# Block-causal attention with a SoLU MLP: transposed tiles placed in an order that alternates partition halves, queries and keys loaded for two head pairs at once, and W_out's rows permuted

## The chip, the cores and the metric

The kernel runs on one core of a Trainium2 chip. Its time is the device time of one execution in microseconds (us). The engines are PE (matrix products and transposes through the identity), DVE, ACT and POOL (elementwise work and reductions) and SP, whose only work here is to issue DMAs, one after the other, in the order of its queue.

## The reference

Attention over 8 batches, 8 heads, 576 positions of 64 channels, with a mask by blocks of 64; then, per token, an MLP with a SoLU and a layer norm. All is float32, and the weights are handed over as float64 words.

```python
scores = scale * np.matmul(q, k.transpose(0, 1, 3, 2))       # scale = 1/8
scores = np.where(block_i >= block_j, scores, -1000000000.0)
attn = softmax(scores)                                        # rows, with 1e-9 in the divisor
x = np.matmul(attn, v).transpose(0, 2, 1, 3).reshape(4608, 512)
h = x @ w_in                                                  # 512 -> 1024
solu = h * softmax(h)
ln = (solu - mean) / np.sqrt(var + 1e-06) * g_ln              # over the 1024
out = ln @ w_out                                              # 1024 -> 512
```

## The kernel before

**Tiling.** The 64 (batch, head) pairs are worked on two heads at a time: 32 "pairs" p, four to a batch. One head lies in partitions 0 to 63, the other in 64 to 127. After every batch the 128-token MLP tiles t that are complete are added, 36 in all. Products that need more than one pass of the reduced float32 format are split into a high and a low part: `qh, ql, kh, kl` for queries and keys, `wih, wil, woh, wol` for the weights, `xh, xl` and `ch, cl` for what the MLP multiplies.

**One pair.** Queries and keys come in raw as `qz, kz`. For pairs 0 to 3 PE transposes them; from pair 4 on (28 pairs) they are loaded as 32-column pieces of 128 bytes (L432, four DMAs for each of q and k), DVE transposes the 32x32 blocks into `qt, kt` (L474), ACT or POOL makes the high part (L475), DVE or POOL the low part (L478, L481). POOL copies the last block's queries into `qdh, qdl` (L485). PE makes the scores (L515, L509), DVE their row maxima (L540), ACT the exponentials into `pb` (L552), DVE the reciprocal sums (L562, L563), POOL or ACT the scaling (L570, L572). Then `pb` must be transposed: for pairs 0 to 3 by PE (L496), from pair 4 on by DVE in 32x32 blocks (L579) and sixteen DMAs (`place`, L584) that carry block row a of quarter r to quarter r of `pt`, 100 KB each. PE multiplies by the values (L596, the "AV" product, 52 matrix instructions a pair) into `xt`.

**One MLP tile.** Two groups of 12 matrix products with 512 columns (L673), maximum, exponential, product with h (L679 to L681), subtraction of the mean in place in `ub` (L683 on POOL or L684 on DVE), square sum (L685), then the transpose: for tiles 4 to 34 by DVE in 32x32 blocks into `zb` (L703), a DMA to DRAM (`zd`, L704) and one back (`ct`, L705); for tiles 0 to 3 and 35 by PE straight from `ub` (L721). High and low parts (L711 to L715), two groups of 12 products with W_out (L733), scaling (L737), the store (L739).

**Weights.** At the start sixteen pieces (eight of W_in, eight of W_out) are loaded as float64 words into `ub` (L345), turned into float32 and split (L347 to L365), with `zb`, `ct` and `ob` as scratch.

**What sets the order.** `Schedule.run` plans all engines at once: each operation has a duration, a priority out of `PARAMS`, and sometimes a choice of engines (`alts`); a list scheduler with slots for PSUM tiles gives one fixed order per engine. SP's queue is part of it: an operation of SP is a run of DMA issues with a time for the issue, `dma` (the time on the DMA engines, one after the other) and `tail`. On the chip each engine walks its order, waiting by semaphores alone.

## Time and profile before

| | |
|---|---|
| median of three runs | 729.7 us (728.79 to 730.06) |
| the profiled execution | 730.28 us, its span 728.5 us, mean granted TensorE clock 0.970 |
| PE, DVE, ACT, POOL busy | 671.1, 607.4, 495.3, 322.5 us |
| DMA | 125.49 MB, 231547 packets, 70.1% of 16 engines' span on SP's queue |
| `place` | 448 issues of 100 KB, 2.2 us to landing |
| q and k of pairs 4 to 31 | 224 issues of 72 KB, 3.0 and 2.7 us to landing |
| weights | 16 issues of 512 KB, 4.2 and 4.3 us to landing |

A busy PE is counted with matmul ends that are modelled, so that gaps in it are real but short stalls do not show. SP's issues do not count as busy time; how full SP is must be read from the order of its instructions in time.

### The profile page before, as it was taken

To read this page: it belongs to the slowest core of one execution; us is meant where nothing else is said; L and a number is where in the kernel's file an instruction comes from. 1 tells how busy PE (TensorE), PEld (TensorE's weight loads), DVE (VectorE), ACT (ScalarE), POOL (GpSimd) and SP (SyncE) were. 2 spreads that over 40 slices of the span, in tenths; PEclk is the share of its full clock that TensorE was granted. 3 is DMA by queue.
4 is the path that set the end of the run, shared out by engine and by line. 5 is a ranking of instruction groups with operands and counts; after the bars stand their busy time and mean duration, and the time that the engine had idled before them with its cause. 6 is when DMAs were issued, how large, how long until landed. Compare 5 with 4: busy or idle time off the path is not lost.

```text
span 728.5 us, 14348 instructions
## 1 busy us (share of the span) xinstructions
PE 671.1 (92%) x4543; PEld 528.1 (72%) x4543; DVE 607.4 (83%) x1262; ACT 495.3 (68%) x1265; POOL 322.5 (44%) x491
## 2 busy tenths in 40 slices
PE   7786968999999998999999999899899988999997
PEld 6566757777677776778777777677677766878886
DVE  6999999988888999789799888899888789755672
ACT  5989958877777777665777686578585658434342
POOL 3755744454444655244353654245454434214310
PEclk7899989999999999999999999999999999999999
DMA  9584676676788888888778888888787874543431
GB/s 236 130 175 118 150 178 117 126 170 146 161 201 201 205 196 193 198 192 210 182 193 197 203 196 173 190 199 196 193 209 178 190 197 110 170 151 130 145 131 57
DMA packets 231547, 125.49 MB, mean 172 GB/s; under 512 B 190640, under 2 KB 206512, under 8 KB 231472
## 3 DMA queue, kind: packets, MB, share of 16 engines
q1 hardware_dynamic: 230416, 124.32, 70.1%
q8 instruction: 36, 0.59, 0.4%
q10 hardware_dynamic: 1056, 0.26, 0.2%
q14 instruction: 39, 0.32, 0.2%
HBM read 52.96 MB, written 25.69 MB: 108 GB/s over the span
## 4 chain that ended last, share of the span: by engine, by line
PE 32%; DVE 23%; SPq 14%; DMA 12%; ACT 12%; issue 5%; POOL 1%; DVEq 0%; ACTq 0%; POOLq 0%
PE ps L733 12%; SPq L584 11%; PE ps L673 9%; PE ps L596 5%; DVE pb L579 5%; DVE nm L540 5%; DMA pt<-pb 4%; ACT pb L552 4%; PE ps L515 4%; DMA ct<-zd 3%; ACT pb L572 3%; SPq L432 2%; DVE ub L681 2%; DVE zb L703 2%; PE ps L509 1%
## 5 line engine op out<-in xcount | busy, mean ns | idle before, releaser
L552 ACT ACTIVATE pb<-ps,nm 128x384 f32<-128x384 f32 (+4 forms) x288 | 157.3, 561 | 69.6 <-DVE nm L540 54.2
L540 DVE TENSOR_REDUCE nm<-ps 128x1 f32<-128x384 f32 (+4 forms) x288 | 131.8, 506 | 0.3
L596 PE MATMUL ps<-pt,vr 128*64 128x128 f32 (+2 forms) x1664 | 104.3, 286 | 25.4 <-DMA pt<-pb 13.7
L596 PEld LDWEIGHTS ps<-pt,vr 128*64 128x64 f32 x1664 | 90.2, 146 | 46.9 <-issue 16.4
L572 ACT ACTIVATE pb<-pb,rz 128x128 f32<-128x128 f32 (+4 forms) x191 | 101.2, 595 | 25.4 <-DVE rz L563 23.0
L579 DVE STREAM_TRANSPOSE pb<-pb 128x1536 f32<-128x1536 f32 (+1 forms) x56 | 102.1, 1829 | 9.5 <-POOL pb L570 5.8
L570 POOL TENSOR_SCALAR pb<-pb,rz 128x384 f32<-128x384 f32 (+4 forms) x97 | 62.3, 652 | 71.3 <-DVE rz L563 30.4
L733 PE MATMUL ps<-woh,ch 128*128 128x512 f32 x288 | 81.6, 405 | 4.0 <-ACT pb L552 3.4
L673 PE MATMUL ps<-wih,xh 128*128 128x512 f32 x288 | 83.8, 413 | 0.2 <-ACT xh L648 0.2
L673 PE MATMUL ps<-wil,xh 128*128 128x512 f32 x288 | 79.4, 398 | 0.0
L733 PE MATMUL ps<-woh,cl 128*128 128x512 f32 x288 | 78.7, 395 | 0.0
L673 PE MATMUL ps<-wih,xl 128*128 128x512 f32 x288 | 78.6, 395 | 0.0
L733 PE MATMUL ps<-wol,ch 128*128 128x512 f32 x288 | 78.6, 394 | 0.0
L733 PEld LDWEIGHTS ps<-woh,ch 128*128 128x128 f32 x288 | 51.8, 188 | 20.2 <-ACT pb L552 5.6
L703 DVE STREAM_TRANSPOSE zb<-ub 128x1024 f32<-128x1024 f32 x31 | 62.5, 2017 | 2.6 <-POOL ub L683 1.4
L673 PEld LDWEIGHTS ps<-wil,xh 128*128 128x128 f32 x288 | 54.8, 190 | 13.0
L673 PEld LDWEIGHTS ps<-wih,xh 128*128 128x128 f32 x288 | 51.1, 190 | 17.3 <-issue 4.8
L673 PEld LDWEIGHTS ps<-wih,xl 128*128 128x128 f32 x288 | 54.3, 188 | 12.8
L733 PEld LDWEIGHTS ps<-woh,cl 128*128 128x128 f32 x288 | 54.3, 188 | 12.8
L515 PE MATMUL ps<-kh,qh 64*128 64x384 f32 (+3 forms) x256 | 57.8, 390 | 6.2 <-ACT pb L552 1.8
L733 PEld LDWEIGHTS ps<-wol,ch 128*128 128x128 f32 x288 | 54.2, 188 | 12.7
L712 POOL TENSOR_SCALAR ch<-ct 128x512 fp32r<-128x512 f32 x36 | 22.0, 620 | 90.0 <-DMA ct<-zd 77.0
(116 smaller groups left out, 1262.3 us busy)
## 6 DMA issues: line engine op xcount, KB each, us to landing
pt<-pb SPq DMA_DIRECT2D x448, 100.0 KB, 2.2
zd<-zb SPq DMA_DIRECT2D x31, 512.0 KB, 3.0
ct<-zd SPq DMA_DIRECT2D x31, 512.0 KB, 4.3
out_dram<-ob SPq DMA_DIRECT2D x36, 256.0 KB, 3.1
vr<-in_v_dram SPq DMA_DIRECT2D x64, 128.0 KB, 3.3
kz<-in_k_dram SPq DMA_DIRECT2D x112, 72.0 KB, 2.7
qz<-in_q_dram SPq DMA_DIRECT2D x112, 72.0 KB, 3.0
ub<-in_moe_w_in_dram SPq DMA_DIRECT2D x8, 512.0 KB, 4.2
```

Source lines behind the costliest of these rows:

```text
L515: PE.matmul(PS(sps[h])[:, off : off + 128 * (i_ + 1)], w_[half[h], 128 * i_ : 128 * i_ + 128], x_[half[h], 0 : 128 * (i_ + 1)], start=n_ = ...
L540: op("DVE", t_dve(wid[u]), lambda sp=sp, off=off, u=u: DVE.tensor_reduce(out=nm_[u], in_=PS(sp)[:, off : off + wid[u]], axis=AX.X, op=ALU. ...
L552: ACT.activation(dst, src, AF.Exp, bias=nm_[u], accum_out=z_[zg][:, zc : zc + 1])
L570: op("POOL", 0.836 * nn + 243, lambda b=b, zg=zg, zc=zc: POOL.tensor_scalar(out=puv(pb, b, pep), in0=puv(pb, b, pep), scalar1=rz_[zg][:, z ...
L572: ("ACT", t_act(nn, 93), lambda b=b, zg=zg, zc=zc: ACT.activation(puv(pb, b, pep), puv(pb, b, pep), AF.Copy, scale=rz_[zg][:, zc : zc + 1] ...
L579: op("DVE", 1.058 * 128 * (s1 - s0) + 86, lambda s0=s0, s1=s1: DVE.transpose(pb[:, :, s0:s1, :], pb[:, :, s0:s1, :]), r=[("P", i, b) for b ...
L584: SP.dma_start(pt_[32 * r_ : 32 * r_ + 32, a_, :, :], pb[32 * a_ : 32 * a_ + 32, r_, :, :])
L596: PE.matmul(dst(PS(av)[half[h]]), vt[:, j, 64 * h : 64 * h + 64], pt_[:, a0:a1, sl, :], start=start, stop=stop)
L673: PE.matmul(o_, a_[:, c, :], w_[:, c, s_], start=(si == 0 and c == 0), stop=(si == 2 and c == NKI - 1))
L703: op("DVE", t_dve(DFF), lambda: DVE.transpose(zb.rearrange("p (r c i) -> p r c i", r=4, i=32), u.rearrange("p (c i r) -> p r c i", r=4, i= ...
L712: alts=[("POOL", 671, lambda c_=c_, h_=h_: POOL.tensor_scalar(out=h_, in0=c_, scalar1=1.0, scalar2=1.0, op0=ALU.mult, op1=ALU.mult), K["a_ ...
L733: PE.matmul(o_, a_[:, c, :], w_[:, c, :], start=(hf == 0 and si == 0 and c == 0), stop=(hf == 1 and si == 2 and c == 7))
```

## The change

Five things change in the code, and all numbers of the planner with them, so that every engine's order is new.

1. **Loads of q and k.** `qz, kz` hold two pairs side by side. One DMA brings 32 columns of two heads: four DMAs of 144 KB for each of q and k per two pairs (L450), 112 issues in all where there were 224. To make the source regular, a pair is now heads 4a+z and 4a+z+2, so W_in's rows are permuted alike: its pieces are loaded in two halves of 64 partitions (`heads`, 16 issues for 8). The 32x32 transposes of q and k are done in place (`qt, kt` are gone): the next load of two pairs must wait until both pairs are through with the raw tile.
2. **Placing.** The sixteen DMAs of `place` are the same, in another order: source and target quarter now change between partitions 0-63 and 64-127 from one DMA to the next.
3. **W_out's rows.** They are loaded with rows r of four interleaved (`rows`, 32 issues for 8, and 4 for 1 of `gt`), so that the DVE transpose of the MLP reads 32 neighbouring elements where it read every fourth. For tiles 0 to 3 and 35, which PE transposes, the subtraction of the mean writes into `zb` in the permuted order; it waits, at tile 0, for all weights, whose scratch `zb` is.
4. **The planner.** A DMA now occupies the modelled DMA engines from its issue on, SP stops when more than 2.5 us are outstanding, `place` has 5.5 us on the DMA engines where it had 0.25, and three durations are larger.
5. **Choices of engine.** With the new numbers, POOL scales 156 of the `pb` blocks (97 before) and ACT 132 (191 before); POOL makes 34 of the 56 high parts of q and k, of which ACT made all; in the weights' preparation DVE makes 7 of the low parts (16 before) and none of the high parts (9 before), and 16 of the clamps (7 before).

```diff
-    "nd": 2, "ld": 63.8, "lv": 26.1, "q": -25.0, "qe": -924.4, ...
+    "nd": 2, "ld": 15.5, "lv": 976.7, "q": 13.1, "qe": 1200.3, ...
...
-                    done = dmafree = max(done, dmafree) + best.dma
+                    dmafree = max(t + min(best.dur, 600.0), dmafree) + best.dma
+                    engfree[e] = max(done, dmafree - DEPTH)
+                    done = max(engfree[e], dmafree)
...
-    qz, kz, qt, kt = (sb(x, [S]) for x in ("qz", "kz", "qt", "kt"))
+    qz, kz = (sb(x, [2, S]) for x in ("qz", "kz"))
...
-    w_in_w = w_in.bitcast(U32).rearrange("(c p) (n t) -> p c n t", p=P, t=2)
-    w_out_w = w_out.bitcast(U32).rearrange("(c p) (n t) -> p c n t", p=P, t=2)
+    w_in_w = w_in.bitcast(U32).rearrange("(a h z d) (n t) -> d a z h n t", h=2, z=2, d=64, t=2)
+    w_out_w = w_out.bitcast(U32).rearrange("(c r j) (n t) -> r j c n t", r=4, j=32, t=2)
...
+    def rows(dst, src):
+        for r_ in range(4):
+            SP.dma_start(dst[r_::4], src[r_])
+
+    def heads(dst, src):
+        for h in range(2):
+            SP.dma_start(dst[64 * h : 64 * h + 64], src[:, h])
...
-                for g in range(4):
-                    dma.dma_start(
-                        dst[32 * g : 32 * g + 32, :].rearrange("p (g d) -> p g d", d=32),
-                        src[b0, 2 * hp + g // 2, :, 32 * (g % 2) : 32 * (g % 2) + 32].rearrange("(g p) d -> p g d", p=32),
-                    )
+            def load2(nm=nm, src=src, dst=dst):
+                for g in range(4):
+                    SP.dma_start(
+                        dst[32 * g : 32 * g + 32].rearrange("p m (g d) -> p (m g) d", d=32),
+                        src[b0, ha + g - g % 2 : ha + g - g % 2 + 2, :, 32 * (g % 2) : 32 * (g % 2) + 32].rearrange("m (g p) d -> p (m g) d", p=32),
+                    )
...
+            elif zs == 0:
+                op("SP", 2600, load2, w=[(nm, 0), (nm, 1)], key=lk, tail=1700, dma=3740)
...
-            op("DVE", t_dve(S) + 30, lambda z=z, t=t: DVE.transpose(t, z), r=[x + "z"], w=[x + "t"], key=kk)
+            op("DVE", t_dve(S) + 30, lambda z=z: DVE.transpose(z, z), r=[zk], w=[zk], key=kk)
...
-            for r_ in range(4):
-                for a_ in range(4):
+            for d_ in (2, 3, 0, 1):
+                for a_ in (0, 2, 1, 3):
+                    r_ = a_ ^ d_
                     SP.dma_start(pt_[32 * r_ : 32 * r_ + 32, a_, :, :], pb[32 * a_ : 32 * a_ + 32, r_, :, :])
...
+        if not PET <= t < PEL:
+            dst, src = (x.rearrange("p (c a b) -> p c a b", a=a_, b=P // a_) for x, a_ in ((zb, 32), (u, 4)))
+            src = src.rearrange("p c r j -> p c j r")
+            cw, ck = ["zb"], "zb"
...
-            op("DVE", t_dve(DFF), lambda: DVE.transpose(zb.rearrange("p (r c i) -> p r c i", r=4, i=32), u.rearrange("p (c i r) -> p r c i", r=4, i=32)), ...
+            op("DVE", t_dve(DFF), lambda: DVE.transpose(zb.rearrange("p (r c i) -> p r c i", r=4, i=32), u.rearrange("p (c r i) -> p r c i", r=4, i=32)), ...
```

How SP's queue reads in the middle of the program, before. A row is a run of equal DMAs: line, what is written and read, the shape of one, how many. `pt<-pb` is `place`, `zd` and `ct` are the two halves of an MLP transpose, `vr` the values.

```order
L584 DMA pt_94<-pb_92 32x800 x16
L704 DMA zd<-zb 128x1024
L739 DMA out_dram<-ob_137 128x512
L432 DMA kz<-in_k_dram 32x18x32 x4
L432 DMA qz<-in_q_dram 32x18x32 x4
L705 DMA ct<-zd 128x4x256
L584 DMA pt_93<-pb_91 32x800 x16
L704 DMA zd<-zb 128x1024
L441 DMA vr_84<-in_v_dram 128x4x64 x2
L445 DMA vr_84<-in_v_dram 64x2x64
L739 DMA out_dram<-ob_138 128x512
L432 DMA kz<-in_k_dram 32x18x32 x4
```

The same place with the change, two pairs of `place` apart:

```order
L608 DMA pt_92<-pb_90 32x800 x16
L744 DMA zd<-zb 128x1024
L779 DMA out_dram<-ob_138 128x512
L450 DMA kz<-in_k_dram 32x36x32 x4
L745 DMA ct<-zd 128x4x256
L450 DMA qz<-in_q_dram 32x36x32 x4
L608 DMA pt_91<-pb_89 32x800 x16
L744 DMA zd<-zb 128x1024
L779 DMA out_dram<-ob_137 128x512
L463 DMA vr_82<-in_v_dram 128x4x64 x2
L467 DMA vr_82<-in_v_dram 64x2x64
L745 DMA ct<-zd 128x4x256
```

Eight issues of q and k now stand between every second pair of `place`, where eight stood between each two; the rest of a turn is as it was. The load stands ahead of a `place` in the queue.

The start of SP's queue, before (the keys of pair 0 go by ACT's queue):

```order
L345 DMA ub_128<-in_moe_w_in_dram 128x1024
L426 DMA kq<-in_k_dram 64x2x64
L421 DMA qz<-in_q_dram 128x4x64 x2
L426 DMA kq<-in_q_dram 64x2x64
L345 DMA ub_129<-in_moe_w_in_dram 128x1024
L441 DMA vr_83<-in_v_dram 128x4x64 x2
```

and with the change:

```order
L352 DMA ub_126<-in_moe_w_in_dram 64x1024 x2
L352 DMA ub_127<-in_moe_w_in_dram 64x1024 x2
L463 DMA vr_82<-in_v_dram 128x4x64 x2
L467 DMA vr_82<-in_v_dram 64x2x64
L463 DMA vr_81<-in_v_dram 128x4x64 x2
L467 DMA vr_81<-in_v_dram 64x2x64
L352 DMA ub_126<-in_moe_w_in_dram 64x1024 x2
L352 DMA ub_127<-in_moe_w_in_dram 64x1024 x2
L443 DMA kq<-in_k_dram 64x2x64
L438 DMA qz<-in_q_dram 128x4x64 x2
```

The queries of pair 0 stood behind two issues; now fifteen stand ahead of them, two of which reuse a weight buffer and so wait for its first piece to be read. On PE, 28 groups of 12 MLP products stand behind the last AV product before, and 33 with the change.

More of the change, by code (lines that the diff above doesn't have):

```diff
@@ L33 @@
 PEP = (0, 1, 2, 3)
+DRP = ()
+PDMA = 5500
 PET, PEL = 4, 35
@@ L38 @@
 SWITCH = 70.0
+DEPTH = 2500.0
 SLACK = 120.0
@@ L278 @@
     zd = dp.tile([P, DFF], F32, name="zd")
+    pd = [dp.tile([P, 4, NSL * 32], F32, name=f"pd{i}") for i in range(2)]
     ct = sb("ct", [4, NKO, 32])
@@ L344, in prep @@
         kr_, k1, k2, k3 = ("ub", i % 2), ("w1", i % 2), ("w2", i % 2), ("ob", i % 2)
-        op("SP", 640, lambda: SP.dma_start(raw, src), w=[kr_], key=key, tail=2700, dma=1270)
+        if gcol is None:
+            op("SP", 2 * 640, lambda: heads(raw, src), w=[kr_], key=key, tail=2700, dma=1270)
+        else:
+            op("SP", 4 * 640, lambda: rows(raw, src), w=[kr_], key=key, tail=2700, dma=1270)
         high = raw[:, :, 1].bitcast(F32)
@@ L372 @@
             s_ = slice(hf * 512, hf * 512 + 512)
[L373 removed]
+            prep(n, w_in_w[:, c // 2, c % 2, :, s_, :], wih[:, c, s_], wil[:, c, s_], None, f"wi{c}_{hf}", K["w0"] + K["w1"] * n)
             n += 1
     for c in range(NKO):
[L376 removed]
+        prep(n, w_out_w[:, :, c], woh[:, c, :], wol[:, c, :], gt[:, c : c + 1], f"wo{c}", K["w0"] + K["w1"] * n)
         n += 1
@@ L414, in attention, with load @@
         pep = p in PEP
+        zs = p % 2
+        ha = 4 * (hp // 2) + zs
         for nm, src, dst in (("kz", k, kz), ("qz", q, qz)):
-            def load(nm=nm, src=src, dst=dst):
+            def load(nm=nm, src=src, dst=dst[:, zs]):
                 dma = ACT if p == 0 and nm == "kz" else SP
-                if peq:
-                    for h in range(2):
-                        dma.dma_start(
-                            dst[:, 0:512].rearrange("p (c d) -> p c d", c=4)[:, :, 64 * h : 64 * h + 64],
-                            src[b0, 2 * hp + h, 0:512, :].rearrange("(c p) d -> p c d", p=P),
-                        )
-                    r0 = 0 if nm == "kz" else 64
+                for h in range(2):
+                    dma.dma_start(
+                        dst[:, 0:512].rearrange("p (c d) -> p c d", c=4)[:, :, 64 * h : 64 * h + 64],
+                        src[b0, ha + 2 * h, 0:512, :].rearrange("(c p) d -> p c d", p=P),
+                    )
+                r0 = 0 if nm == "kz" else 64
+                SP.dma_start(
+                    kq[r0 : r0 + 64, :].rearrange("p (h d) -> p h d", h=2),
+                    src[b0, ha : ha + 3 : 2, 512:576, :].rearrange("h p d -> p h d"),
+                )
+            def load2(nm=nm, src=src, dst=dst):
+                for g in range(4):
@@ L521, in attention @@
             else:
-                d, md = sum(3 * t_row(128 * (i_ + 1)) for i_, _ in us) + {1: 0, 2: 48, 3: 74}[us[0][0]], 2
+                d, md = sum(3 * t_row(128 * (i_ + 1)) for i_, _ in us) + {1: 90, 2: 48, 3: 74}[us[0][0]], 2
                 rd = [(x, iq) for x in ("kh", "kl", "qh", "ql")] + [(x, iq, 0) for x in ("qh", "ql")]
@@ L581, in place, with back @@
         def place():
-            for r_ in range(4):
-                for a_ in range(4):
+            for d_ in (2, 3, 0, 1):
+                for a_ in (0, 2, 1, 3):
+                    r_ = a_ ^ d_
                     SP.dma_start(pt_[32 * r_ : 32 * r_ + 32, a_, :, :], pb[32 * a_ : 32 * a_ + 32, r_, :, :])
         ptk = [("pt", p % NPT, c0) for c0, _ in ptc]
-        if not pep:
-            op("SP", 16 * 633, place, r=[("T", i, 0), ("T", i, 1)] + [("P", i, u) for u in units], w=ptk, key=p + K["pe" + sfx], tail=1500, dma=250)
+        tk = [("T", i, 0), ("T", i, 1)] + [("P", i, u) for u in units]
+        if p in DRP:
+            pd_ = pd[p % 2]
+            def back():
+                for r_ in range(4):
+                    SP.dma_start(pt_[32 * r_ : 32 * r_ + 32, :, :, :].rearrange("p a s i -> p a (s i)"), pd_[:, r_, :].rearrange("(a p) n -> p a n", a=4))
+            op("SP", 630, lambda: SP.dma_start(pd_, pb.rearrange("p r s i -> p r (s i)")), r=tk, w=[("pd", p % 2)], key=p + K["pe" + sfx], tail=1700, dma=4000)
+            op("SP", 4 * 560, back, r=[("pd", p % 2)], w=ptk, key=p + K["pe" + sfx], tail=1700, dma=4000)
+        elif not pep:
+            op("SP", 16 * 633, place, r=tk, w=ptk, key=p + K["pe" + sfx], tail=1500, dma=PDMA)
         kk = p + K["av" + sfx]
```

59 lines of the change are left out of this document (28 added, 31 removed), and 12 rows, old and new, of the table PARAMS.

## The prediction

> **What bounds the kernel now.** I read the page's shares first, then the span in three stages, then who makes PE wait, then SP's queue, because SP does not count as busy.
>
> ```profile
> PE 671.1 (92%) x4543; PEld 528.1 (72%) x4543; DVE 607.4 (83%) x1262; ACT 495.3 (68%) x1265; POOL 322.5 (44%) x491
> ...
> PE 32%; DVE 23%; SPq 14%; DMA 12%; ACT 12%; issue 5%; POOL 1%; DVEq 0%; ACTq 0%; POOLq 0%
> PE ps L733 12%; SPq L584 11%; PE ps L673 9%; PE ps L596 5%; DVE pb L579 5%; DVE nm L540 5%; DMA pt<-pb 4%; ACT pb L552 4%; PE ps L515 4%; DMA ct<-zd 3%; ACT pb L572 3%; SPq L432 2%; DVE ub L681 2%; DVE zb L703 2%; PE ps L509 1%
> ```
>
> PE is busy for 92% of the span, so at most 728.5 - 671.1 = 57.4 us lie in gaps on PE, unless short stalls hide in its modelled ends. In the chain that ended last, issuing `place` alone (L584) holds 11%, as much as the largest group of matrix products. The windows say where the gaps are:
>
> ```profile
> 0.00:200.00 200.00, 169.10 (x1275) 132.71 (x1277) 177.17 (x408) 160.05 (x419) 103.65 (x165) 0.91 0.68 155
> 200.00:645.00 445.00, 422.74 (x2926) 331.43 (x2926) 383.11 (x776) 301.61 (x787) 198.63 (x297) 0.99 0.79 190
> 645.00:728.50 83.50, 79.24 (x344) 63.93 (x344) 47.13 (x78) 33.63 (x60) 20.23 (x30) 1.00 0.33 117
> ```
>
> Columns: PE, its weight loads, DVE, ACT, POOL, then granted clock, DMA share, GB/s. Up to 200 us PE idles 30.9 us, with DVE 89% busy (weights and softmax share it) and the clock at 0.91. From 200 to 645 PE idles 445.00 - 422.74 = 22.3 us. After the last AV product PE has nothing but MLP groups and is full: 4.3 us idle, nearly all of it the last store. So a gain in the middle has 22.3 us to take, and this is what PE and SP wait for there:
>
> ```profile
> PE ps L596 <- DMA pt<-pb: 12.5, 6, 4.3
> PE ps L733 <- ACT pb L552: 3.4, 3, 2.3
> ...
> SPq L739 <- ACT ob L737: 8.2, 3, 5.1
> SPq L704 <- DMA ct<-zd: 6.8, 2, 3.7
> ```
>
> The AV product waits for the placed tile, 12.5 of the 22.3 us; SP itself waits little in 445 us. One full turn of SP's queue, from one `zd` to the next:
>
> ```profile
> 307.17 0.53 SPq L704 DMA_DIRECT2D zd<-zb  x1
> 307.80 0.40 SPq L739 DMA_DIRECT2D out_dram<-ob  x1
> 308.25 2.64 SPq L432 DMA_DIRECT2D qz<-in_q_dram  x4
> 310.93 2.13 SPq L432 DMA_DIRECT2D kz<-in_k_dram  x4
> 313.16 0.45 SPq L705 DMA_DIRECT2D ct<-zd  x1
> 313.70 1.01 SPq L441 DMA_DIRECT2D vr<-in_v_dram  x2
> 314.76 0.66 SPq L445 DMA_DIRECT2D vr<-in_v_dram  x1
> 315.52 10.69 SPq L584 DMA_DIRECT2D pt<-pb  x16
> 326.31 0.53 SPq L704 DMA_DIRECT2D zd<-zb  x1
> ```
>
> 19.14 us, of which 18.51 are issuing. SP is the tightest queue of the middle, PE is close behind it (95%), DVE third (86%).
>
> **Part 1, the loads of q and k: SP's turn gets shorter.** In this turn they cost 2.64 + 2.13 = 4.77 us for eight issues, 0.53 to 0.66 each. Four are left per pair. An issue that describes 36 pieces a partition instead of 18 has no row. From below it costs 0.53 (the number of pieces does not matter), from above 1.3, twice 0.66 (it is all that matters). For the first end speaks that issues of very different make cost alike here: 0.67 for one of `place` (10.69 / 16, one piece a partition), 0.53 to 0.66 for 18 pieces. I take 0.65: 2.6 us a pair, 2.2 less, and SP's turn falls from 19.1 to 16.9 us. The upper end (5.2 us) would give back all of it. PE's busy time per turn is 0.95 x 19.14 = 18.2 us, so PE, not SP, then sets the pace, and what it gains is not 2.2 us a turn but its own gaps: the 12.5 us of AV waits, and half of the other 9.8, since those waits end on ACT and DVE chains that get only some relief (part 3): **17.4 us**. Bounds: 22.3 if all gaps close, 0 if AV waits as before.
>
> The new load waits until both pairs are through with the raw tile, and `place` stands behind it in the queue, then AV behind `place`. The tile was free after the transpose; now it is free after the high and low parts too:
>
> ```profile
> L474 DVE STREAM_TRANSPOSE kt<-kz 128x576 f32<-128x576 f32 x28 | 21.6, 770 | 3.3 <-DMA kz<-in_k_dram 3.0
> L475 ACT ACTIVATE kh<-kt 128x576 fp32r<-128x576 f32 x28 | 19.2, 685 | 1.6 <-PE ps L515 1.5
> L481 POOL TENSOR_TENSOR kl<-kt,kh 128x576 fp32r<-128x576 f32 x25 | 35.8, 1434 | 21.9 <-ACT kh L475 21.7
> ```
>
> That is 0.69 + 1.43 = 2.1 us later, once in two pairs, with 2 x 16.9 us in which it may fall. The cover is that slack; if it is gone, 14 loads x 2.1 us = 29 us. I take one such wait in all, **+2**.
>
> **Part 2, the order inside `place`.** The same 16 issues at the same 0.67 us. 100 KB each 0.67 us is about 150 GB/s, and in the middle the DMA engines are 79% busy while moving 190 GB/s in all; the issue sets the pace, not the transfer, so I take **0**. If the halves do collide today, the landing after the last issue and the waits for a full queue get shorter; that is in the better rival. The Trainium skill speaks against that hope (SBUF — State Buffer, section "Can I just issue two DMAs to hit both halves?"): it answers no, the two run one after the other on the same engines, with 6% measured for it. By that rule the better rival loses one of its three supports.
>
> **Part 3, the transposes of the MLP on DVE.** Today they read every fourth element:
>
> ```profile
> L703 DVE STREAM_TRANSPOSE zb<-ub 128x1024 f32<-128x1024 f32 x31 | 62.5, 2017 | 2.6 <-POOL ub L683 1.4
> L579 DVE STREAM_TRANSPOSE pb<-pb 128x1664 f32<-128x1664 f32 x28 | 53.1, 1896 | 3.2 <-POOL ch L712 1.6 <-ACT pb L572 1.5
> L579 DVE STREAM_TRANSPOSE pb<-pb 128x1536 f32<-128x1536 f32 x28 | 49.3, 1761 | 6.3 <-POOL pb L570 5.8 <-ACT pb L572 0.2 <-DMA pt<-pb 0.2
> ```
>
> The contiguous ones cost (1896 - 1761) / 128 = 1.055 ns an element, so 1024 elements 1761 - 512 x 1.055 = 1221 ns. 0.80 us saved 31 times is 24.7 us of DVE. Little of it is on the path: the chain gives L703 2% of 728.5, 14.6 us, of which 40% is 5.8; and a shorter step only moves up the next wait, for `ct`. Between 0 and 5.8 I take **-3**. The Trainium skill (SBUF — State Buffer, the note on SBUF cachelines) says that a stride of up to four float32 is free; read so, the stride of four costs nothing today, the term is 0 and the sum 3 us higher. The rows above, 1.97 ns an element against 1.15, do not agree with that reading.
>
> **Part 4, the start.** The queries of pair 0 are issued behind fifteen others instead of two:
>
> ```profile
> 0.72 0.39 SPq L345 DMA_DIRECT2D ub<-in_moe_w_in_dram  x1
> 1.16 0.74 SPq L426 DMA_DIRECT2D kq<-in_k_dram  x1
> 1.95 1.14 SPq L421 DMA_DIRECT2D qz<-in_q_dram  x2
> ...
> 8.68 0.44 PE L515 MATMUL ps<-kh,qh 64*128 64x384 f32 x2 [0.77 <-ACT qh L395]
> ```
>
> Eight halves of W_in at about 0.45 us with the gap, six of v at 0.57 (1.01 + 0.66 for three, above) and one `kq` at 0.79 make 7.8 us, so `qz` starts at 8.5 instead of 1.95 and the first score comes 6.6 us later. What can hide it is the weights' preparation, which DVE, the fullest engine of this stage, has to do at some time anyway and can do first: cost between 0 and +6.6, I take **+3**. The 35 extra issues of weights and `gt` are 16 us of SP at 0.45; SP has holes for them in this stage:
>
> ```profile
> 54.08 0.61 SPq L445 DMA_DIRECT2D vr<-in_v_dram  x1
> 56.52 0.34 SPq L345 DMA_DIRECT2D ub<-in_moe_w_out_dram  x1
> 65.70 0.37 SPq L441 DMA_DIRECT2D vr<-in_v_dram  x1
> ```
>
> (9 us here.) Cost 0; without the cover each of the eight W_out pieces lands 3 x 0.45 = 1.4 us later, 11 us for the last. Against this, DVE gives up weight work:
>
> ```profile
> L364 DVE TENSOR_TENSOR wil<-zb,wih 128x512 fp32r<-128x512 f32 x4 | 2.8, 696 | 0.0
> L363 DVE CAST wih<-zb 128x512 fp32r<-128x512 f32 x3 | 1.3, 428 | 0.0
> L349 DVE TENSOR_SCALAR zb<-ub 128x512 f32<-128x512 f32 x3 | 1.3, 421 | 3.5 <-DMA ub<-in_moe_w_in_dram 3.5
> ```
>
> Nine low parts less (6.3 us), nine casts less (3.9), nine clamps more (3.8): 6.4 us of DVE's 177. At DVE's 89% I take half, **-3**.
>
> **Part 5, moves without a price.** POOL gets 59 more scalings of `pb` and 34 high parts of q and k:
>
> ```profile
> L572 ACT ACTIVATE pb<-pb,rz 128x128 f32<-128x128 f32 (+4 forms) x191 | 101.2, 595 | 25.4 <-DVE rz L563 23.0
> L570 POOL TENSOR_SCALAR pb<-pb,rz 128x384 f32<-128x384 f32 (+4 forms) x97 | 62.3, 652 | 71.3 <-DVE rz L563 30.4
> ...
> L570 POOL TENSOR_SCALAR pb<-pb,rz 128x512 f32<-128x512 f32 x25 | 17.9, 716 | 20.2 <-DVE rz L563 17.4 <-ACT pt L395 1.5 <-PE ps L733 0.5
> L570 POOL TENSOR_SCALAR pb<-pb,rz 128x640 f32<-128x640 f32 x8 | 6.4, 804 | 0.7 <-DVE rz L563 0.3
> L683 POOL TENSOR_SCALAR ub<-ub,ms 128x1024 f32<-128x1024 f32 x11 | 12.4, 1123 | 22.6 <-DVE ms L682 12.3 <-DVE ms L688 10.0
> ```
>
> 59 x 0.65 + 34 x 0.76 (576 wide, between 716 and 804 ns) is 64 us, which takes POOL from 44% to 53%; each is within 0.1 us of ACT's. POOL's own idle time covers it; if not, 93 x 0.1 = 9 us. The five tiles that PE transposes get their mean subtracted into a scattered `zb`: one such step at 1.1 us (L683, in place) to twice that, five times, partly on the path of tile 0, which also waits for the last weights: 0 to 5.5, I take **+1**. The 33 groups instead of 28 behind the last AV product only move work: PE does them at 79.24 / 28 = 2.83 us each in either place.
>
> **Sum.** 728.5 - 17.4 + 2 - 3 + 3 - 3 + 1 = 711.1 us of span; the profiled execution lies 730.28 - 728.5 = 1.8 above its span, which makes 712.9, and the median of the runs shown is 0.6 below that execution: **712 us**.
>
> **Rivals.**
>
> - *PE's gaps close all over* (better). `place` lands sooner with the halves apart, SP has air, and DVE's 25 us come through. Then 22.3 in the middle, 5.8 for the MLP transposes and 6.4 at the start: 729.7 - 34.5 = 695. For it: SP, DVE and ACT all get less work. Against: three engines at 86 to 97% in the middle always collide somewhere.
> - *The wait changes its name.* An issue of 36 pieces costs near 1.3 us, SP's turn stays at 19 us, AV goes on waiting for `pt<-pb`, and only parts 3 and 4 stay: 729.7 - 3 + 3 - 3 = about 727. For it: issues of q in this very turn already cost 0.66, more than the 0.53 of k right behind them, so something holds them up. That the change does not do what it says would look the same.
> - *The shared raw tile stops SP* (slower). The load of the next two pairs reaches the head of SP's queue before the second pair's low parts are done, and holds `place` behind it. It decides from where it holds SP longer than the 4.4 us that two pairs save. If the transposes, high and low parts of k and of q come one behind the other, 2 x (0.77 + 0.69 + 1.43) = 5.8 us, every load of two pairs loses 5.8 - 4.4 = 1.4 us: 729.7 + 14 x 1.4 = 749. For it: 21.7 us of POOL's idle time before L481 are waits for `kh`, so this chain does run late. Against: two turns give 34 us of room, and in the queue the load stands behind a whole `place`.
>
> **How the numbers follow.** The forecast with its own range of 703 to 721 has 0.53; the better rival 0.18; the unchanged wait 0.13; the slower one 0.16. A difference under 0.2% (1.5 us) cannot be told from none here: of the unchanged wait's 0.13 about a third falls in it, and a little of the slower one's, so same 0.05, faster 0.80, slower 0.15. The range takes the better rival's value as its low end, 693, and reaches up to where the slower one begins, 732.
>
> **What would show it.** Right: AV's wait for `pt<-pb` well under 12.5 us between the tenth and the last pair, a run of four loads near 2.6 us, holes in SP's turn, transposes `zb<-ub` near 1.2 us, first score near 15 us. Wrong: runs of four loads at 5 us; SP waiting for `kl` or `ql` ahead of a load; PE's idle time before 200 us well over 31 us.

## The result, and the profile after: 1.7% slower

| | before | changed |
|---|---|---|
| median | 729.75 us (728.79 to 730.06) | 742.05 us (740.99 to 743.43) |
| ratio | | 1.0172, 95% interval [1.0152, 1.0192] |
| span of the profiled execution | 728.5 us | 741.6 us |
| PE busy | 671.1 us | 671.6 us |
| idle time of PE | 57.4 us | 70.0 us |

712 us was forecast. PE is busy for as long as before, within 0.5 us, so nearly all of the loss is idle time of PE. Three views say where; first the shares and the stages of the changed kernel (columns as before: PE, its weight loads, DVE, ACT, POOL, granted clock, DMA share, GB/s):

```profile
PE 671.6 (91%) x4543; PEld 527.9 (71%) x4543; DVE 576.4 (78%) x1271; ACT 471.7 (64%) x1189; POOL 362.9 (49%) x558
...
0.00:200.00 200.00, 160.01 (x1191) 125.61 (x1191) 159.62 (x374) 149.39 (x378) 109.32 (x172) 0.97 0.71 143
200.00:645.00 445.00, 419.19 (x2958) 327.99 (x2954) 367.29 (x810) 287.60 (x752) 233.26 (x355) 0.98 0.86 195
```

PE now idles 40.0 us before 200 us (30.9 before) and 25.8 us from 200 to 645 (22.3), so 9.1 + 3.5 = 12.6 of the 13.1 us by which the span grew. DVE has 31 us less to do and ACT 24, and no time comes of it. The tenth AV product ends at 215.3 us (199.9), the last at 644.0 (644.7): between these two the changed kernel is 16 us quicker, but it puts 88 groups of 12 MLP products there instead of 96, and the 33 groups left over follow at 2.83 us each. At that price, and with 23 groups done before the tenth AV product instead of 20, the same work takes about 6.9 us longer up to the tenth AV product and about 6.5 us longer from there to the last (an estimate: 15.4 - 3 x 2.83 and 8 x 2.83 - 16.1). So the loss lies about half in the start and half in the middle.

The waits of PE between 200 and 645 us, of the changed kernel (total, times, longest):

```profile
PE ps L630 <- DMA pt<-pb: 9.0, 7, 2.3
PE ps L630 <- ACT pb L595: 3.7, 2, 2.2
PE ps L538 <- DVE ql L501: 3.0, 2, 1.5
```

and SP's queue over two pairs:

```profile
310.68 0.52 SPq L744 DMA_DIRECT2D zd<-zb  x1
311.31 0.39 SPq L779 DMA_DIRECT2D out_dram<-ob  x1
312.11 1.06 SPq L463 DMA_DIRECT2D vr<-in_v_dram  x2
313.21 0.71 SPq L467 DMA_DIRECT2D vr<-in_v_dram  x1
314.04 0.53 SPq L745 DMA_DIRECT2D ct<-zd  x1
316.99 0.36 SPq L779 DMA_DIRECT2D out_dram<-ob  x1
317.44 10.09 SPq L608 DMA_DIRECT2D pt<-pb  x16
327.63 0.53 SPq L744 DMA_DIRECT2D zd<-zb  x1
328.48 3.21 SPq L450 DMA_DIRECT2D kz<-in_k_dram  x4
331.79 5.48 SPq L450 DMA_DIRECT2D qz<-in_q_dram  x4
337.37 0.77 SPq L745 DMA_DIRECT2D ct<-zd  x1
338.24 10.29 SPq L608 DMA_DIRECT2D pt<-pb  x16
348.63 0.53 SPq L744 DMA_DIRECT2D zd<-zb  x1
```

From `zd` to `zd` 16.95 and 21.00 us, 18.98 on average: the turn is as long as the 19.14 us of before. Over all turns between 200 and 645 us the mean is 19.55 us, and 18.91 before. The AV product still waits for the placed tile, 9.0 us instead of 12.5. Four loads of k cost 3.21 us and four of q 5.48; 2.6 us was forecast for either.

SP as a whole gained little. From the tenth to the last AV product, 22 pairs in both kernels, its issuing takes 379.5 us before and 374.5 with the change. The loads of q and k fall from 92.9 to 78.5 us, but the issues of `place`, `vr` and `ct` together take 10.5 us more.

### The profile page after: what moved, and what is told of

Its sections match the earlier page's. It is cut to its first block, busy times and chain, and to the rows that moved or that the text cites. A ratio compares the mean times of both kernels' runs of the same rounds, so it can differ in the third digit from the quotient of the medians.

```text
span 741.6 us, 14333 instructions
## 1 busy us (share of the span) xinstructions
PE 671.6 (91%) x4543; PEld 527.9 (71%) x4543; DVE 576.4 (78%) x1271; ACT 471.7 (64%) x1189; POOL 362.9 (49%) x558
## 4 chain that ended last, share of the span: by engine, by line
PE 21%; SPq 11%; DVE 10%; DMA 8%; ACT 3%; issue 3%; POOL 2%; DVEq 0%; POOLq 0%; ACTq 0%
PE ps L773 10%; SPq L608 7%; PE ps L707 7%; DMA ct<-zd 4%; DVE pb L602 3%; PE ps L630 3%; SPq L450 2%; DMA qz<-in_q_dram 2%; DVE nm L563 2%; DMA pt<-pb 1%; PE ps L538 1%; ACT pb L575 1%; SPq L463 1%; POOL cl L755 1%; DVE qz L497 1%
## 5 line engine op out<-in xcount | busy, mean ns | idle before, releaser
L575 ACT ACTIVATE pb<-ps,nm 128x128 f32<-128x128 f32 (+4 forms) x288 | 157.6, 567 | 56.6 <-DVE nm L563 40.2
L563 DVE TENSOR_REDUCE nm<-ps 128x1 f32<-128x128 f32 (+4 forms) x288 | 131.9, 507 | 0.4
L630 PE MATMUL ps<-pt,vr 128*64 128x128 f32 (+2 forms) x1664 | 102.7, 283 | 19.6 <-DMA pt<-pb 13.0
L593 POOL TENSOR_SCALAR pb<-pb,rz 128x384 f32<-128x384 f32 (+4 forms) x156 | 92.7, 609 | 52.2 <-DVE rz L586 24.0
L595 ACT ACTIVATE pb<-pb,rz 128x512 f32<-128x512 f32 (+4 forms) x132 | 73.6, 615 | 20.7 <-DVE rz L586 19.7
L686 POOL TENSOR_TENSOR xl<-xt,xh 128x512 fp32r<-128x512 f32 (+1 forms) x40 | 47.7, 1199 | 38.8 <-PE ps L707 13.7
L773 PEld LDWEIGHTS ps<-wol,ch 128*128 128x128 f32 x288 | 54.2, 188 | 12.8
L707 PEld LDWEIGHTS ps<-wih,xl 128*128 128x128 f32 x288 | 54.2, 188 | 12.8
L773 PEld LDWEIGHTS ps<-woh,cl 128*128 128x128 f32 x288 | 54.2, 188 | 12.8
L755 POOL TENSOR_TENSOR cl<-ct,ch 128x512 fp32r<-128x512 f32 x38 | 49.1, 1306 | 26.0 <-ACT ch L751 16.7
```

The costliest lines, as they stand in the source:

```text
L563: op("DVE", t_dve(wid[u]), lambda sp=sp, off=off, u=u: DVE.tensor_reduce(out=nm_[u], in_=PS(sp)[:, off : off + wid[u]], axis=AX.X, op=ALU. ...
L575: ACT.activation(dst, src, AF.Exp, bias=nm_[u], accum_out=z_[zg][:, zc : zc + 1])
L593: op("POOL", 0.836 * nn + 243, lambda b=b, zg=zg, zc=zc: POOL.tensor_scalar(out=puv(pb, b, pep), in0=puv(pb, b, pep), scalar1=rz_[zg][:, z ...
L595: ("ACT", t_act(nn, 133), lambda b=b, zg=zg, zc=zc: ACT.activation(puv(pb, b, pep), puv(pb, b, pep), AF.Copy, scale=rz_[zg][:, zc : zc + 1 ...
L630: PE.matmul(dst(PS(av)[half[h]]), vt[:, j, 64 * h : 64 * h + 64], pt_[:, a0:a1, sl, :], start=start, stop=stop)
L686: POOL.tensor_tensor(out=xl[i][:, :, c0:c1], in0=xt[x][:, :, a0:a1], in1=xh[i][:, :, c0:c1].bitcast(F32), op=ALU.subtract)
```

## The experiments

All ratios are to the kernel before, run on the same chip beside it. Medians of runs from different chips are less comparable: that of the kernel before lies between 729.75 and 733.30 us. Of most edits only the lines that carry them are shown.

### Pieces of the change, one by one

**Pair 0's loads first** (the changed kernel with the loads of q and k of pair 0 at the head of SP's and ACT's queues):

```diff
-        for o_ in sc.run():
+        seq = sc.run()
+        for o_ in [o for o in seq if o.early] + [o for o in seq if not o.early]:
```

> The changed kernel with every engine's order kept, except that the loads of pair 0's queries and keys stand first in SP's and ACT's queues, as they did before the change. Theory A (the late start made the change slow): the first score comes near 9 us instead of 20.5, PE's idle time before 200 us falls from 40.0 to about 31, and the whole is 9 to 12 us faster than the changed kernel, 730 to 733 us. Theory B (the 144 KB loads hold SP and the DMA queues in the middle, and a late start is absorbed because the stage up to 200 us is bound by DVE and ACT): first score near 9 us all the same, but at most 3 us faster, 739 to 742 us.

743.57 us, 1.0148 [1.011, 1.0186]. The loads came early, but ACT's copies of pair 0 still stood behind the weights' steps: first score at 21.8 us. It tested little, so the next run moved all work of the first pairs.

**All of pairs 0 to 3 earlier** (every operation of these pairs up to 12 us ahead, against the weights', on all engines):

```diff
+            rank[o.idx] = (max(0.0, o.t - 12000.0 * max(0.0, 1.0 - o.t / 60000.0)) if o.early else o.t, n_)
+        for o_ in sorted(seq, key=lambda o: rank[o.idx]):
```

> The changed kernel with the attention work of pairs 0 to 3 moved ahead of the weights' preparation by up to 12 us on every engine (loads, copies, scores, softmax; nothing else moves), so that the high parts of pair 0 no longer stand behind four pieces of W_in on ACT. First score near 9 us. Theory A (the start costs about 9 us of PE): ratio to the kernel before falls from 1.017 to about 1.005. Theory B (the stage up to 200 us is bound by what ACT and DVE have to do in all): the tenth AV product still ends near 215 us and the ratio stays above 1.012.

745.59 us, 1.0162 [1.0123, 1.0201]. The first score is at 13.0 instead of 20.5 us (9 was expected), and the tenth AV product still ends at 218 us, as theory B had it. Moving the start forward by 7.5 us buys nothing back.

**The weights' T3 conversions on POOL** instead of ACT, which is fully busy from 80 to 100 us in the changed kernel:

```diff
-            o_.fn()
+            (o_.full["POOL"] if o_.early else o_.fn)()
```

> The changed kernel with the sixteen conversions of the weights' T3 part (L363) on POOL instead of ACT, the order of everything kept. Theory that ACT, fully busy from 80 to 120 us, paces the stage up to 200 us: 16 x 0.5 us of ACT go away, PE's idle time before 200 us falls from 40 to about 33 us and the time by 5 to 8 us, to 734 to 738. Theory that ACT only happens to be full there and that SP's loads or the clock set the pace: 741 to 744, the tenth AV product still at 213 to 217 us.

744.49 us, 1.0176 [1.0138, 1.0213]; PE idles 41.4 us before 200 us. Taking these conversions off ACT buys nothing, so ACT alone does not pace that stage.

**MLP transposes with a stride of four again**, the rest of the changed kernel kept (W_out as stored; the tiles that PE transposes are still centred into `zb`):

```diff
-            SP.dma_start(dst[r_::4], src[r_])
+            SP.dma_start(dst[32 * r_ : 32 * r_ + 32], src[r_])
...
-            dst, src = (x.rearrange("p (c a b) -> p c a b", a=a_, b=P // a_) for x, a_ in ((zb, 32), (u, 4)))
-            src = src.rearrange("p c r j -> p c j r")
+            dst, src = zb, u
...
```

> The changed kernel with W_out's rows in natural order: the MLP transposes read every fourth element again (2.0 us instead of 1.23 us, 31 times, 24.5 us of DVE), and the five tiles that PE transposes copy into zb without a permutation. All orders kept. If the prediction's term of 3 us was right, 744 to 746 us; if DVE is nowhere on the path, 742; if DVE carries more of the middle than I thought, 750 or more.

744.49 us, 1.0171 [1.0125, 1.0218], as without the edit. The group of transposes took 2031 ns each, against these 1231 in the changed kernel:

```profile
L743 DVE STREAM_TRANSPOSE zb<-ub 128x1024 f32<-128x1024 f32 x31 | 38.2, 1231 | 1.6 <-POOL ub L722 1.2
```

So 31 x 0.80 = 24.8 us of DVE are worth nothing that these runs can tell; an interval of 3.4 us to either side does not exclude the 3 us of the prediction. The centring into `zb`, no longer scattered, took 1132 ns on POOL instead of 2162, and that brought nothing either.

**The order of `place`**, alone in each direction: the old one in the changed kernel, the new one in the kernel before.

```diff
-            for d_ in (2, 3, 0, 1):
-                for a_ in (0, 2, 1, 3):
-                    r_ = a_ ^ d_
+            for r_ in range(4):
+                for a_ in range(4):
```

> The changed kernel with the sixteen DMAs of the placing in their old order (one target quarter after the other). If the alternation of partition halves matters, it is slower than the changed kernel's 742 us by 2 us or more, with a longer landing than 2.2 us and packets that take longer; if the issue sets the pace, 742 within 1.5 us.

739.93 us, 1.0115 [1.0075, 1.0155]: perhaps a little better than the new order, with intervals that overlap; neither case had expected that.

> The kernel before with nothing but the new order of the 16 DMAs of place. Theory that the halves collide: SP's queue paces the middle, place is 10.7 of its 19.1 us, and shorter packets (210 ns against 217, 3%) empty the queue sooner, so up to 22 places x 0.3 us = 7 us faster, 723 to 728. Theory that the order is worth nothing: issuing sets the pace, 0.67 us each in either order, and the time is within 0.3% of before, 728 to 732. From the changed kernel with the old order, which was 0.6% faster than with the new one, a loss of up to 4 us would follow, 734.

730.46 us, 0.9996 [0.9973, 1.002]: no difference. The median landing of one `place` DMA between 200 and 600 us falls from 2.56 to 2.21 us and its packets of 3200 bytes from 217 to 210 ns, and issuing stays at 0.62 us each. The Trainium skill (SBUF — State Buffer, section "Can I just issue two DMAs to hit both halves?") answers no and states +6% for two DMAs at once, one on either half, over a single one. That is another measure than packet times, but the 3% and the unchanged total here agree with its answer.

### What paces the middle

**Two-pair loads as two DMAs of 72 KB each**:

```diff
-                    SP.dma_start(
-                        dst[32 * g : 32 * g + 32].rearrange("p m (g d) -> p (m g) d", d=32),
+                    for mm_ in range(2):
+                        SP.dma_start(
+                            dst[32 * g : 32 * g + 32, mm_].rearrange("p (g d) -> p g d", d=32),
```

> The changed kernel with each load of two pairs issued as sixteen DMAs of 72 KB at the same place in the queue instead of eight of 144 KB. If the cost of an issue is the time that its packets take in the DMA queue (B), eight more issues cost next to nothing: 16 issues take about as long as the 8 took (7.9 us for k and q), and the time stays at 742 within 3 us. If the cost is per issue, SP's turn grows by 8 x 0.55 = 4.4 us per two pairs, 14 times, and up to 60 us come on top: 760 to 800 us.

758.7 us, 1.0353 [1.0332, 1.0375]. Between 200 and 600 us a small issue costs 0.60 (k) and 0.63 us (q), a large one 0.82 and 1.21; sixteen small ones take 9.9 us of SP where eight large ones take 8.1, and packets of 128 bytes take 13.3 ns on average in the small and 16.9 in the large ones. Halving the count therefore saves 1.8 us per two pairs and not 4.4. The result lies between the two theories: against the kernel before the loss grows from 12.3 to 26.3 us, 14 us for 14 x 1.8 = 25 us more issuing of these loads.

**No loads of q from pair 8 on** (both kernels then use old queries, so part of the input is left out):

```diff
             def load2(nm=nm, src=src, dst=dst):
+                if nm == "qz" and p >= 8:
+                    return
```

> The changed kernel without the loads of the queries from pair 8 on: the output is made from stale queries, all other work and every order are kept. It takes 4.8 us per two pairs off SP's queue. If SP's queue sets the pace of the middle (theory C), the 22 pairs between the tenth and the last AV product take 390 to 405 us instead of 429, and the whole is 20 to 35 us faster. If PE's fixed interleaving or DVE sets it, under 6 us.

> The kernel before without the loads of the queries from pair 8 on (stale queries, all else kept): 2.5 us of SP's 19 per pair. Theory C: the middle was paced by SP before the change too, and with 96 MLP groups between the tenth and the last AV product PE's floor is near 400 to 420 us against 445 measured: 15 to 30 us faster. If PE paced it, under 5 us.

Changed: 717.75 us, 0.9782 [0.9745, 0.9819]. Before: 711.32 us, 0.9694 [0.9663, 0.9725]; its waits of the AV product for the placed tile fall from 12.5 to 1.2 us:

```profile
PE ps L598 <- DMA pt<-pb: 1.2, 2, 0.6
```

So SP's queue, or the transfers behind it, or the waits for q's loads themselves, do pace the middle of both, as the prediction had it for SP; the run takes out all three at once. Without these loads the changed kernel is 6.4 us slower than the kernel before instead of 12.3, each median with an interval of about 2.7 us to either side.

**The same loads issued by ACT**, in the kernel before and in the changed one (its edit is shown):

```diff
+                dma = ACT if p >= 8 and nm == "qz" else SP
```

> The kernel before with the loads of q, from pair 8 on, issued by ACT instead of SP; the same bytes and packets. Theory that SP's issue time paces the middle: 24 pairs x 4 x 0.63 us = 60 us leave SP's queue, and the time nears that of the kernel without these loads (711), 712 to 722; ACT, which holds 69% of the middle, has room. Theory that the DMA engines' time for 128-byte packets paces it: 728 to 734, with SP's issues of place longer than 0.62 us each. Should ACT be hurt by standing behind its own issues: above 734.

790.07 us, 1.0794 [1.0758, 1.083]. SP's `place` now waits 69.5 us between 150 and 645 us, by the profile for these loads.

> The changed kernel with the two-pair loads of q, from pair 8 on, issued by ACT instead of SP. Theory that SP's issue time paces the middle: 12 loads x 4.8 us = 58 us leave SP, and the time nears that of the changed kernel without these loads (718), 719 to 728, the middle 410 to 418 us instead of 429. Theory that the DMA engines' packets pace it: 739 to 744. Should ACT stand 5 us behind each of its own loads and delay the exponentials by that, 12 x 5 = 60 us at most are lost and the time is above 745.

767.38 us, 1.0474 [1.0432, 1.0515]. In both the third case of the expectation came, ACT and what depends on it are hurt by its own issues: in the first run the AV product waits 47.9 us for the placed tile although SP has fewer issues. The likely reason is that the load has to wait for its raw tile, and that on ACT everything behind it (exponentials, scaling, the copies) waits too; no run separates it. These two runs therefore say nothing on SP against packets.

### Operations against order

Since no piece alone gave the loss back, the question was whether the operations or the order that was planned for them carry the loss.

**The changed kernel planned with the old numbers and the old DMA model, and the kernel before planned with the new numbers** (the table of 65 numbers exchanged; in the first also the DMA model and three durations, in the second the table alone):

> The changed code with all of the planner's old numbers (priorities, durations, no model of a full DMA queue): tells the code's change from the new numbers. If the new code is good and the new numbers are bad, it is at or under the kernel before, 715 to 730 us; if the loads of two pairs at once and the in-place transposes are what costs, it is as slow as the changed kernel or slower, 740 us or more.

> The kernel before, planned with the changed kernel's numbers. If the numbers only fit the operations for which they were chosen, as the old numbers on the changed kernel did (772), 740 to 770. If the numbers carry little, 728 to 735.

772.05 us, 1.0512 [1.0466, 1.0557], and 749.47 us, 1.0253 [1.021, 1.0296]. Each code is best with its own numbers. An order that fits badly costs some 26 us on the changed kernel and 18 on the kernel before, more than the change itself.

**Operations and order exchanged**: each kernel's operations, replayed in the other's recorded order, engine by engine.

```diff
-        for o_ in sc.run():
+        for o_ in sc.replay():
```

> The changed kernel's operations, every one, in the order of the kernel before on each engine, with that kernel's choice of engines and PSUM buffers; the loads of two pairs stand where the load of the first of them stood, or as soon behind as their raw tile is free. Theory that the loss lies in the order: PE's idle time before 200 us falls from 40 to 31 us or less, the tenth AV product ends near 200 us, and the time is 718 to 731. Theory that the loss lies in the operations themselves (two-pair loads 3.3 + 4.8 us of issue, packets of 16.9 ns): 738 to 750, tenth AV product at 212 us or later.

> The other corner: the operations of the kernel before (loads of one pair, tiles kt and qt, W_out as stored, MLP transposes with a stride of four, old order of place) in the order of the changed kernel; the load of a second pair follows as soon as the first pair's raw tile is transposed. Theory that the loss lies in the order: 738 to 750. Theory that it lies in the operations: 724 to 733.

804.17 us, 1.0996 [1.0949, 1.1043], and 806.01 us, 1.1013 [1.098, 1.1046]. Neither expectation allowed for both. The changed operations do not fit the old order at all: 73 us; nor do the old operations the new one: 75 us. A replay thus shows what operations cost in an order that was not made for them, which can be much more than they cost in their own. That made the old order a good place to look for what had got worse, since nothing there had been arranged around it. Three runs undid parts of the change inside e13:

**One pair per load again**, into two raw halves in turn:

```diff
-                op("SP", 2600, load2, w=[(nm, 0), (nm, 1)], ...
+                op("SP", 2040, load2, w=[(nm, zs)], ...
```

> As e13 (the changed kernel's operations in the order of the kernel before), but each pair loads its own half of the raw tile by itself, four DMAs of 72 KB, as the kernel before did; a half is free for a whole pair longer than there. Theory that the shared raw tile makes the loss: the 50 us that SP waits ahead of the loads go, the stretch from the tenth to the last AV product falls from 477 to about 445 us, and the time to 760 to 775; to about 735 if the loads cause the 42 us before the tenth as well. Theory that the scattered zb makes it: at most 10 us less than e13's 804.

**W_out as stored**, transposes with a stride of four, tiles 0 to 3 and 35 centred in place, so that tile 0 no longer waits for the weights:

```diff
-        if not PET <= t < PEL:
+        if False:
...
-        cz = u if PET <= t < PEL else zb
+        cz = u
```

> As e13, but with W_out's rows as stored, the MLP transposes with a stride of four, and the first and last tiles centred in place instead of into zb, all as in the kernel before; the two-pair loads stay. Theory of the scattered zb: the 42 us before the tenth AV product go (from 242 to about 200 us) and the time falls to 755 to 770. Theory of the shared raw tile: it stays above 790.

**Both undone**:

> Both undone, still in the order of the kernel before: what is left of the change are the in-place transposes of q and k with two raw halves in turn, the order of place, and the weights' loads in two and four DMAs. If the two causes explain e13, 724 to 735; if the raw halves in turn give SP air (5.8 us of waiting for kt there), 722 to 728, faster than before. Above 745 a third cause is left.

| in the order of the kernel before | median | ratio | against before |
|---|---|---|---|
| e13: all changed operations | 804.17 us | 1.0996 [1.0949, 1.1043] | +73.0 us |
| e18: the two-pair loads kept | 790.63 us | 1.0803 [1.0768, 1.0838] | +58.6 us |
| e17: W_out's permutation kept | 751.53 us | 1.0271 [1.024, 1.0303] | +19.5 us |
| e19: neither | 732.54 us | 1.0004 [0.9981, 1.0027] | +0.6 us |

The two nearly add up (58.6 + 19.5 = 78 against 73), and without them nothing is left that these runs can tell: the in-place transposes (with two raw halves in turn), the new order of `place` and the split weight loads together cost 0.6 us, within 1.7. The theory of the shared raw tile held for e18 (above 790) and was short of the truth for e17 (760 to 775), which gained more. The theory of the scattered `zb` gave the 42 us before the tenth AV product to `zb` alone: that product ends at 242.5 us in e13, at 223.0 in e17, 224.8 in e18 and 202.2 in e19, so that each cause has about half of it.

How the two-pair load costs time is seen in e18's queues. SP, POOL and DVE around one load:

```profile
390.94 1.42 POOL L714 TENSOR_TENSOR kl<-kz,kh 128x576 fp32r<-128x576 f32 x1 [0.50 <-ACT kh L708]
392.39 3.29 SPq L660 DMA_DIRECT2D kz<-in_k_dram  x4
398.39 0.78 DVE L707 STREAM_TRANSPOSE kz<-kz 128x576 f32<-128x576 f32 x1 [2.56 <-DMA kz<-in_k_dram]
400.20 0.73 DVE L711 SCALAR_TENSOR_TENSOR ql<-qz,qh 128x576 fp32r<-128x576 f32 x1
401.00 2.45 SPq L660 DMA_DIRECT2D qz<-in_q_dram  x4
407.30 0.78 DVE L707 STREAM_TRANSPOSE qz<-qz 128x576 f32<-128x576 f32 x1 [5.76 <-DMA qz<-in_q_dram]
```

The low part `kl` of the old pairs ends at 392.36 and the load is issued at 392.39; `ql` ends at 400.93, and its load starts at 401.00. DVE keeps its order and waits for what has just been asked for. From 150 to 645 us DVE waits for these loads, in e18, in the changed kernel's own order and in the kernel before:

```profile
DVE kz L707 <- DMA kz<-in_k_dram: 37.9, 8, 7.5
DVE qz L707 <- DMA qz<-in_q_dram: 10.5, 3, 5.8
```

```profile
DVE qz L497 <- DMA qz<-in_q_dram: 6.7, 5, 3.8
DVE kz L497 <- DMA kz<-in_k_dram: 4.4, 3, 2.1
```

```profile
DVE kt L474 <- DMA kz<-in_k_dram: 3.0, 2, 2.7
DVE qt L474 <- DMA qz<-in_q_dram: 1.4, 1, 1.4
```

48.4 us in e18, 11.1 in the changed kernel and 4.4 in the kernel before. PE's largest wait of e18 between 200 and 645 us is that of the scores for `ql`, the step that ends this chain for the queries:

```profile
PE ps L748 <- DVE ql L711: 13.4, 4, 5.4
```

The changed kernel's own order hides most of it. In the turn shown above the load of k leaves, here too, when `kl` ends (327.01 + 1.44 = 328.45 and 328.48):

```profile
327.01 1.44 POOL L504 TENSOR_TENSOR kl<-kz,kh 128x576 fp32r<-128x576 f32 x1
...
328.48 3.21 SPq L450 DMA_DIRECT2D kz<-in_k_dram  x4
```

That holds for five of the 13 loads of k that follow another one; the other eight leave 0.3 to 7.7 us after `kl`, and those of q 0.3 to 12.6 us after `ql`, when SP's order comes to them.

Before, the loads of k lie complete 6.2 us ahead of their transpose (median of 28 pairs, up to 16 us), those of q 2.8 us; in the changed kernel it is 0.75 and 0.3 us (medians of 14 loads), in e18 0.1 and 1.0. In e18 the shared raw tile took that lead: up to 645 us SP waits there 18.3 us for `ql` and 12.7 for `kl` ahead of a load. In the changed kernel's order the lead is as short, but the raw tile alone does not explain it: a load of 144 KB also takes longer to land, 4.2 us for k and 5.0 for q where 72 KB took 2.7 and 3.0. No run loads two pairs into a second raw tile, which would tell the late release from the longer load.

The permutation's 19.5 us lie at the start. The tiles that PE transposes are now centred into `zb`, a scratch tile of the weights. In e17:

```profile
146.56 0.65 DVE L592 TENSOR_TENSOR wol<-zb,woh 128x512 fp32r<-128x512 f32 x1
...
147.30 2.43 POOL L934 TENSOR_SCALAR zb<-ub,ms 128x1024 f32<-128x1024 f32 x1 [4.01 <-DVE wol L592]
...
161.34 2.07 PE L985 MATMUL ps<-woh,ch 128*128 128x512 f32 x4 [0.69 <-ACT ch L976]
```

The centring of tile 0 begins when the last weight piece has left `zb`, at 147.3, and the first product with W_out comes at 161.3. In the kernel before it comes at 126.3, before the weights are done, since tile 0 needs only its own `ub`:

```profile
114.87 1.13 POOL L683 TENSOR_SCALAR ub<-ub,ms 128x1024 f32<-128x1024 f32 x1 [3.29 <-DVE ms L688]
...
126.26 1.16 PE L733 MATMUL ps<-woh,ch 128*128 128x512 f32 x4
```

In the changed kernel's own order the first such product is at 142.2 us. The new order makes up for part of it by finishing the weights sooner, at 132 instead of 146 us.

## Why the prediction was wrong

The price was wrong by 30 us, and the sign with it. By its terms: between 200 and 645 us PE's idle time was to fall by 17.4 - 2 = 15.4 us, and it rose by 3.5; before 200 us the terms came to 3 - 3 + 1 = 1, and it rose by 9.1; the 3 us of the transposes did not come. That is 18.9 + 8.1 + 3 = 30 us. The step that failed first is the largest term, the -17.4; two others had been written down as small.

- **"-17.4" for PE's gaps (part 1): the step that failed.** SP's turn was to get 2.2 us shorter, 48 us over 22 pairs; SP's issuing fell by 5.0 us. The price of an issue, 0.65 us, is 0.82 for k and 1.21 for q, inside the bounds of 0.53 to 1.3 and at the end that I did not take, and other issues got longer by 10.5 us, for which there was no term. So the turn did not get shorter, the AV product still waits 9.0 of its 12.5 us, and PE's other waits grew from 9.8 to 16.8 us. The rival "the wait changes its name" had this step right. That the number of pieces does not matter is refuted by the split loads, as far as a load with twice the pieces and twice the bytes can show it. Where to look was right: in e9, without q's loads, the AV waits that were to close do close.
- **"+2" for the shared raw tile (part 1).** The dependence was seen, down to the 2.1 us by which the tile comes free later, and "two turns of room" were taken as cover. But the delay was not the price. Before, a load could be issued as soon as the raw tile was transposed, a pair ahead; now it can only start after the last low part of the second pair, and the same engines need it at once. What goes is the lead, from 6.2 to 0.75 us for k, and in the order of the kernel before, with nothing rearranged, the two-pair loads cost 58.6 us. What they cost in the changed kernel's own order is not known. The rival "the shared raw tile stops SP" had the right dependence and the right sign, and its 749 us was 7 us too high for the changed kernel. That it came so near is luck: SP waits for `kl` only 3.6 us in all up to 645 us in the changed kernel, not 1.4 us at every load.
- **"+1" for the scattered centring (part 5).** The step was sized rightly, 2162 ns each, within the 1.1 to 2.2 us given:

```profile
L722 POOL TENSOR_SCALAR zb<-ub,ms 128x1024 f32<-128x1024 f32 x4 | 8.6, 2162 | 4.0 <-PE ps L761 4.0
```

  Its wait was not: tile 0 waits for all the weights' scratch. The sentence named that wait and gave it no price; in the old order the permutation with it is worth 19.5 us. That the wait costs and not the writing fits e4, where the writing is short, the wait stays and the time is the same.
- **"0" for the halves (part 2)**: right, by e3. **"-3" for the transposes (part 3)**: 1221 ns was forecast and 1231 measured, so the size was right. The Trainium skill (SBUF — State Buffer, the note on SBUF cachelines) says that a stride of up to four float32 is free; 2031 ns in e4 with a stride of four against 1231 contiguous do not agree. The worth on the path, forecast as 3 us, is nil within the runs' uncertainty.
- **"+3" for the start (part 4).** The first score came at 20.5 us, not 15: I followed SP's queue and left out ACT's, where the load of pair 0's keys, and the copies after it, moved behind steps of the weights; e1 moves the loads alone, and the first score stays at 21.8 us. The wait for these keys is PE's longest before 200 us in the changed kernel:

```profile
PE ps L483 <- DMA kz<-in_k_dram: 12.2, 1, 12.2
```

  But e6 shows that moving it forward by 7.5 us buys nothing back.
- **"-3" for DVE's relief (part 4)**: DVE is 17.6 us less busy before 200 us, and PE idles more.
- Of the signs named for the reading, loads of 3.2 and 5.5 us and 40 us idle before 200 us were on the side of "wrong". Holes in SP's turn were to show that the forecast holds; in the two turns shown there are 4.0 us of them, where the turn of before had 0.6, and it did not hold.

What stays open: how the 12 us of the changed kernel divide between these causes, and whether all of them come from these causes. Its order was planned around the two-pair loads and the permutation, so that undoing one inside that order is no test; they were measured apart only in the old order, which was not made for them and where they cost more. That the planner simply found a less good order for the changed kernel is not excluded: numbers that fit badly cost 18 and 26 us in e16 and e7. That the start's 9.1 us come from tile 0's wait is argued from 126.3 against 142.2 us, not shown; the first product with W_out comes late in e18 too, at 147.0 us, where tile 0 does not wait for the weights, and early in e16, at 123.9 us, where the tenth AV product still ends at 218.9. No version tried beats the kernel before with all of its work done: e3 and e19 equal it.

## What to carry to other kernels

Ask of a larger load what it does to the *lead* of that load: sharing a buffer between two steps moves its release behind the last reader of the second, and a load that was ready a step ahead can become one that arrives when it is needed. And price the whole queue, not the issues that go away: here 14.4 us of loads were saved and 10.5 us came back in other issues. A dependence that one has written down needs a price in what it keeps from starting, not in how long the instruction takes. And where a fixed order is fitted to the operations, test a change by replaying the old order with parts of the change undone; in the new order the cost is spread over every engine and single pieces seem innocent. The replay finds which operations matter; its sizes are those of an order that does not fit (804 us here, where the planned order takes 742).

## What the runs showed of the hardware

- Between 200 and 600 us one DMA of 144 KB in pieces of 128 bytes held SP for 0.82 us (k) and 1.21 us (q) on average in the changed kernel, half as large a one for 0.60 and 0.63 in e5. In e18, whose order issues the loads of k and q apart, it was 0.73 and 0.83, so the time of an issue is not fixed by its size. The packets of 128 bytes took 16.9 ns on average in the changed kernel and 12.8 in the kernel before; the median is 13 ns in both.
- In the slowest versions PE also ran at a lower granted clock: 0.927 with PE busy 87% of the span (e13), 0.940 at 88% (e18), 0.981 at 93% (e19). Close by there is no such order (0.970 at 92% before, 0.983 at 91% with the change), and which of the two follows from the other was not tested. From 200 to 645 us, e18 and then e19, with the same matrix products in all:

```profile
200.00:645.00 445.00, 405.14 (x2745) 316.79 (x2744) 353.47 (x732) 286.44 (x750) 192.54 (x287) 0.95 0.78 177
```

```profile
200.00:645.00 445.00, 425.48 (x2978) 334.11 (x2975) 388.51 (x785) 303.36 (x791) 200.00 (x298) 0.99 0.79 192
```

  Over the whole span the same 4543 matrix instructions keep PE busy for 696.0 us in e18 and 672.8 in e19, at mean clocks of 0.940 and 0.981. Of the 62.6 us by which e18's span is longer than the kernel before's (PE busy 671.1 us), 24.9 are PE being busy longer.
